# Projecting q and k in blocks of 128 columns, with DMAs that place the heads

## The chip, the cores and the metric

The kernel runs on one core of a Trainium2 chip. The metric is the device time of one execution in microseconds (us). In the core, TensorE (PE in the profile) multiplies matrices, ScalarE (ACT) takes exponentials, VectorE (DVE) and GpSimd (POOL) do elementwise work, and SyncE (SP) only issues DMAs. PSUM, where matmuls write, has eight banks of 128 x 512 fp32. Each engine works through its own instructions in a fixed order and waits on semaphores where it needs another's result.

## The reference, cut to what matters

```python
# x: 2048 x 640, 32 heads of 20
q, k, v = split(x @ wqkv)
o = softmax(q @ k.T / sqrt(20)) @ v          # per head, 2048 x 2048 scores
a = o @ wo
h = x @ w1 + b1                              # 2048 x 1536
b = (h * tanh(softplus(h))) @ w2             # "mish"
g = sigmoid((x * gate_w).sum(-1))
out = g * a + (1 - g) * b
```

The exponentials of the scores, 32 x 2048 x 2048, are by far the most elementwise work.

## The kernel before

The whole instruction order is written by a planner in Python. `Plan.add` (line 91) appends an instruction to an engine and keeps an estimated clock for each engine from the costs given (a DMA counts as done 2.0 us after its issue, line 45). Where the code decides what comes next, it does so by these estimated clocks; what comes out is a fixed program.

**Attention.** The work is cut into units (query chunk c of 512, group g of 4 heads, key tile kt of 128, head j). Three units make a slot; there are 683 slots, and the main loop (line 1037) has one step for each. A step issues the exponential of its slot (`emit_e`, line 738, the ACT row L749), the scores of the slot two ahead (`emit_s`, line 715, L723), and products with v of older slots (`pv`, L822). A score matmul needs the exponential of two slots before to have left its banks. Keys and queries of a group lie in `KT` and `QT` as four heads of 20 rows, each padded to 32 rows, so that a head starts at a row divisible by 32. One group of 512 queries takes 16 key tiles, 21 1/3 slots. The first chunk of queries, c = 0, takes slots 0 to 170 and is called stage one below.

**Off units.** In some slots the third unit's exponential is taken off ACT: DVE evicts the scores (L763) and computes the exponential with a polynomial (L776 to L780). `choose` (line 788) picks them where DVE's queued work is small.

**Repeats.** Where PE would be busy for too small a share of a step, `repeat_s` (L733) issues the score matmuls a second time, to the same place.

**Fillers.** All other matmuls are tasks that share one PSUM bank, `FB`: each has some matmuls and then an eviction, almost always on DVE, which frees the bank. `tasks` is ordered by due step. A forced task whose due step has come is issued at the head of the step; otherwise, at the end of each step, `pick` (line 1002) may give a task that is ready, as long as PE's estimated clock stays within the end of the next exponential (line 1074). It gives nothing while the bank is not free at PE's estimated clock.

- `kq_task(k, g, c)`: q (k = 0) or k (k = 1) of group g for 512 rows of x: 5 matmuls of 512 columns (L402) with a weight in which the group's 80 columns are padded to 128. POOL or DVE copy the padded weights (`pad`, L391). One DVE cast (L422) writes the result to `QT` or `KT`, already in padded rows. There are 64 of them; k of all rows and q of the first chunk are due in stage one. k of chunk c is due 3 steps before the first slot that reads it.
- `v_task(g, c)`: v of a group, 20 small matmuls (L437), cast by L445; 32 of them, all in stage one.
- `sq_task(n)`: the guard. POOL squares x and the weights (L478), PE sums them over the rows (L491), DVE takes the maximum (L498). From the eight maxima a flag is set that decides whether a second, safe program has to run (it doesn't here). Due at steps 60 to 165.
- `h_task`, `b_task`, `p_task`: the dense branch and the output projection, from slot 171 on; `mish` between them uses ACT (L574), DVE and POOL. An `h_task` can start only when all eight sums are read, because they share the buffer `HB`.

**Norm.** When a group ends, DVE evicts the sums (L884) and SP issues three DMAs one after the other: `RR<-OUNG` (L887), after a reciprocal `SUMS<-RR` (L892), then `BCT<-SUMS` (L894), which spreads the reciprocals over the rows. DVE multiplies (L864) when that has landed.

**Start.** SP issues four transposing loads of x, one per 512 rows (L354). ACT issues the loads of the weights: the first group's columns at once, the others after the first part of x has landed. q and k of group 0 and chunk 0 are projected, the scores of slots 0 and 1 follow.

Of the kernel before, what the change touches and what calls it, by code (L numbers as in the profile page):

```python
# [166 lines left out]
def bass_gated_mix__softmax_full_mha__dense_activation_mish__prompt_kernel(  # L167
# [71 lines left out]
    PADK = REG[:, NFT * (2 * D + 2):].rearrange("p (b f c) -> p b f c", b=2, c=P)  # L239
# [12 lines left out]
    PADQ = WOQ[:, NFT * D:NFT * (D + 2 * P)].rearrange("p (b f c) -> p b f c", b=2, c=P)  # L252
# [20 lines left out]
    def attention(pl, fast):  # L273
# [70 lines left out]
        if fast:  # L344
# [17 lines left out]
            m_padq = pl.add("dve", lambda e: e.memset(PADQ, 0.0), cost=0.4)  # L362
            m_padk = pl.add("dve", lambda e: e.memset(PADK, 0.0), cost=0.4)
# [17 lines left out]
            pad_done, pad_read = {}, {}  # L381

            def pad(k, g, again):

                if (k, g, again) not in pad_done:
                    b = g % 2
                    src = (WQ, WK)[k][:, :, g * HD:(g + 1) * HD].rearrange("p f (j d) -> p f j d", d=DH)
                    dst = (PADQ, PADK)[k][:, b, :, :].rearrange("p f (j d) -> p f j d", d=32)[:, :, :, 0:DH]
                    load = w_load[("wq", "wk")[k] + ("0" if g == 0 else "")]
                    pad_done[(k, g, again)] = pl.add(  # L390
                        "dve" if g == 0 and not again else "pool", lambda e: e.tensor_copy(dst, src),  # L391
                        [(m_padq, m_padk)[k], load, pad_read.get((k, b))], cost=0.4 if g == 0 else 1.2)
                    (wq_read, wkv_read)[k].append(pad_done[(k, g, again)])
                return pad_done[(k, g, again)]

            def kq_task(k, g, c, due, forced=True):
                b = g % 2
                dst = (QT, KT)[k]
                pads = (PADQ, PADK)[k]

                def mm(f):
                    return lambda e, bank: e.matmul(  # L402
                        PS[:, bank, :], pads[:, b, f, :], xt(c)[:, f, :], start=(f == 0), stop=(f == NFT - 1))

                def finish(bank, last):
                    pad_read[(k, b)] = last
                    x_read[c].append(last)
                    (wq_read, wkv_read)[k].append(last)

                    if c == ((0, 1, NC - 1, NC - 1)[c] if k == 0 else NC - 1):  # L410
                        if g + 2 < NG:
                            pad(k, g + 2, min(c, 2) if k == 0 else 0)
                        elif k == 0 and c < 2:
                            pad(0, g + 2 - NG, c + 1)
                    first = k == 1 and g == 0 and c == 0
                    to = dst[:, g, c * CW:(c + 1) * CW]
                    if first:
                        h = CW // 2
                        ev = pl.add("act", lambda e: e.copy(to[:, 0:h], PS[:, bank, 0:h]), [last], cost=0.4)
                        k_more.append(pl.add("act", lambda e: e.copy(to[:, h:], PS[:, bank, h:]), [last], cost=0.4))  # L420
                    else:
                        ev = dve(lambda e: e.tensor_copy(to, PS[:, bank, :]), [last], 0.69)  # L422
                    (q_done, k_done)[k][(g, c)] = ev

                    if first:
                        return k_more[0]
                    return ev

                return Task([mm(f) for f in range(NFT)], PASS, finish, due,
                            lambda: [xt_load[c], pad(k, g, min(c, 2) if k == 0 else 0)], forced)  # L430

# [35 lines left out]
            def sq_src(n):  # L467
                return xt(n) if n < 4 else (WQ, WK)[(n - 4) // 2][:, :, n % 2 * HALF:(n % 2 + 1) * HALF]

            def square():  # L470
# [6 lines left out]
                after = [xt_load[n]] if n < 4 else [w_load[k] for k in (("wq", "wq0"), ("wk", "wk0"))[(n - 4) // 2]]  # L477
# [3 lines left out]
                if n >= 4:  # L481
                    (wq_read, wkv_read)[(n - 4) // 2].append(op)
                else:
                    x_read[n].append(op)

            def sq_task(n, due):

                w = CW if n < 4 else HALF
# [22 lines left out]
            def load_w1(n):  # L511

                k = n % 6
                assert len(sq_ops) == 8
# [4 lines left out]
            def load_w2():  # L519
                flush(lambda: "busy" not in ei_free.values())  # L520
                w2_load.append(pl.add("sp", lambda e: e.dma_start(
                    W2, B_w2.rearrange("(f p) c -> p f c", p=P)), [*ei_free.values()], "w2", cost=0.6))

            def load_wo():
                assert len(sq_ops) == 8
# [189 lines left out]
        def emit_s(s):  # L715
# [3 lines left out]
            for i, (c, g, kt, j) in enumerate(slots[s]):  # L719
                need = deps + ([k_done[(g, kt // 4)], q_done[(g, c)]] if fast else [])  # L720
# [34 lines left out]
        def emit_x(s):  # L755
# [8 lines left out]
                s_op[s], ei_free[b], *(wkv_read if c == 1 and g == 0 and n < 3 else ())], EVICT)  # L764
# [137 lines left out]
        if fast:  # L902
            pad(0, 0, 0)
            pad(1, 0, 0)
            for task, bank in [(kq_task(0, 0, 0, -1), 3), (kq_task(1, 0, 0, -1), 4)]:
# [9 lines left out]
            for c in range(1, NC):  # L915
                due = slot_of(0, 0, 4 * c)
                tasks.append(kq_task(1, 0, c, due - 3))
                tasks.append(v_task(0, c, due - 1))
            for g in range(1, NG):
                due = slot_of(0, g, 0)  # L920
                tasks.append(kq_task(0, g, 0, due - 5))
                for c in range(NC):
                    due = slot_of(0, g, 4 * c)
                    tasks.append(kq_task(1, g, c, due - 3))
                    tasks.append(v_task(g, c, due - 1))
            start = slot_of(1, 0, 0)
            last_kv = tasks[-1]
            for n in range(8):
                t = sq_task(n, 60 + 15 * n)
# [11 lines left out]
            qs = [(kq_task, (0, g, 1)) for g in range(NG)]  # L941
            qs += [(kq_task, (0, g, c)) for g in range(NG) for c in range(2, NC)]
# [19 lines left out]
            for t, (make, args) in zip(made, rest):  # L962
# [4 lines left out]
                if make is kq_task:  # L967
                    t.due = min(t.due, slot_of(args[2], args[1], 0) - 4)
# [12 lines left out]
        def flag_ops(last):  # L981
# [5 lines left out]
            a = pl.add("dve", lambda e: e.tensor_tensor(m[:, 0:1], m[:, 0:1], m[:, 1:2], ALU.max), [a])  # L987
            for n in (0, 2, 3):
                a = pl.add("dve", lambda e, n=n: e.tensor_tensor(
                    m[:, 0:1], m[:, 0:1], m[:, n:n + 1], ALU.mult), [a])  # L990
            f = pl.add("dve", lambda e: e.tensor_scalar(
                FLAG[0:1, 0:1], m[:, 0:1], (SAFE / (SCALE * DH)) ** 2, None, ALU.is_gt), [a])
# [9 lines left out]
        def pick():  # L1002

            if now["open"]:
                return now["open"]
            for t in tasks:
                more = t.ready()
                free = bank_free.get(FB)
                if free is not None and free.t1 + HOP + FREE > pl.now["pe"]:
                    return None  # L1010
                if more is not None and all(d is None or safe(d) <= pl.now["pe"] for d in more):
                    return t
# [24 lines left out]
        for step in range(NSLOT + 40):  # L1037
# [22 lines left out]
            if step + 2 < NSLOT:  # L1060
# [5 lines left out]
                if owed + rate > 0.1 and pick():  # L1066
# [9 lines left out]
            while owed > 0 and step < NSLOT:  # L1076
                t = pick()
# [139 lines left out]
```

## Time and profile before

| | |
|---|---|
| median of 3 runs (lowest, highest) | 967.91 us (965.39, 973.04) |
| the profiled execution | 968.21 us, of which 966.4 us are the profile's span |
| ACT busy | 920.5 us, 95% of the span |
| PE busy | 799.7 us, 83% |
| DVE busy | 614.4 us, 64% |
| POOL busy | 397.3 us, 41% |
| granted PE clock, mean | 0.964 |

A row of a group of instructions names the line, the engine, the operation and what it writes and reads; then how often, the sum of busy time and the mean of one instruction in ns; after the bar the idle time of the engine just before these instructions and what ended most of it. Instructions overlap in their pipelines: the mean of one is longer than the pace at which they follow each other. The five matmuls of a `kq_task`, at 395 ns each, pass in 1.25 us.

### The profile page before, as it was taken

The numbers are of one execution on the slowest core, as the hardware profiler recorded it, in microseconds if no ns is written. First come the engines' busy times: TensorE is split into PE (matmuls) and PEld (weight loads), VectorE is DVE, ScalarE is ACT, GpSimd is POOL, SyncE is SP. The second block draws the span as 40 slices with busy tenths as digits, with TensorE's granted clock in tenths as the row PEclk, the third lists the DMA queues.
The fourth block names the chain that finished last, engine by engine and source line by source line (L and its number), as shares of the span: only waits on it lengthen the run. The fifth ranks groups of instructions, "written<-read, shape, count | busy, mean of one in ns | idle before, by whom it ended". The sixth has DMA issues, their size and how long they took to land.

```text
span 966.4 us, 16483 instructions
## 1 busy us (share of the span) xinstructions
PE 799.7 (83%) x6886; PEld 260.9 (27%) x6886; DVE 614.4 (64%) x1006; ACT 920.5 (95%) x738; POOL 397.3 (41%) x465
## 2 busy tenths in 40 slices
PE   8888889888888888888878888877887888787985
PEld 3332233333222122222222222222222222222221
DVE  2356765565677577656666667775767755757645
ACT  5999999999999889999999999999999999999995
POOL 2400243120266456605355557156556525656100
PEclk9998999999999889999999999999999999999798
DMA  9000000000310111200111111011011011110000
GB/s 211 2 13 13 12 13 2 12 13 26 121 42 27 38 35 44 49 28 25 53 47 46 35 40 39 26 54 51 24 40 53 12 54 33 49 39 13 12 12 31
DMA packets 63137, 35.98 MB, mean 37 GB/s; under 512 B 22225, under 2 KB 59089, under 8 KB 63057
## 3 DMA queue, kind: packets, MB, share of 16 engines
q1 hardware_dynamic: 59040, 32.40, 12.0%
q10 hardware_dynamic: 3936, 2.46, 0.9%
q8 instruction: 56, 0.92, 0.4%
q14 instruction: 25, 0.20, 0.1%
q0 software_dynamic: 80, 0.00, 0.0%
HBM read 29.10 MB, written 2.88 MB: 33 GB/s over the span
## 4 chain that ended last, share of the span: by engine, by line
ACT 67%; PE 13%; DMA 10%; DVE 7%; issue 2%; POOL 1%; ACTq 0%; POOLq 0%
ACT ETS L749 65%; DMA BCT<-SUMS 5%; PE PS L723 4%; DMA SUMS<-RR 3%; PE PS L402 3%; PE PS L822 2%; ACT REG L574 2%; PE PS L543 2%; DVE ER L779 1%; DMA XB<-in_A_x_dram 1%; PE PS L733 1%; DVE OTN L864 1%; DMA RR<-OUNG 1%; PE PS L616 1%; DVE OFF L780 1%
## 5 line engine op out<-in xcount | busy, mean ns | idle before, releaser
L749 ACT ACTIVATE ETS<-PS 128x1536 bf16<-128x1536 f32 (+1 forms) x683 | 905.3, 1541 | 24.8 <-PE PS L723 17.8
L723 PE MATMUL PS<-QT,KT 32*128 32x512 bf16 x2048 | 275.3, 395 | 137.2 <-ACT ETS L749 126.4
L822 PE MATMUL PS<-ETS,V_all 128*21 128x512 bf16 x1980 | 210.3, 396 | 0.9 <-ACT ETS L749 0.9
L723 PEld LDWEIGHTS PS<-QT,KT 32*128 32x128 bf16 x2048 | 67.0, 91 | 360.3 <-ACT ETS L749 331.6
L583 POOL TENSOR_TENSOR T<-REG 128x256 f32<-128x256 f32 x48 | 43.8, 913 | 214.4 <-DVE REG L588 214.4
L779 DVE SCALAR_TENSOR_TENSOR ER<-ER,EM 128x512 f32<-128x512 f32 x136 | 108.4, 797 | 1.9
L583 POOL TENSOR_TENSOR T<-T 128x128 f32<-128x128 f32 x96 | 69.8, 727 | 51.9 <-DVE T L599 46.3
L822 PEld LDWEIGHTS PS<-ETS,V_all 128*21 128x21 bf16 x1980 | 49.3, 89 | 141.2 <-issue 133.6
L733 PE MATMUL PS<-QT,KT 32*128 32x512 bf16 x650 | 85.5, 386 | 0.0
L543 PE MATMUL PS<-XB,REG 128*128 128x256 bf16 x480 | 79.3, 287 | 4.9 <-DVE QT L422 2.6
L583 POOL TENSOR_TENSOR REG<-REG,T 128x256 f32<-128x256 f32 x96 | 79.2, 825 | 7.5
L616 PE MATMUL PS<-W2R,HB 128*128 128x320 bf16 x384 | 77.8, 311 | 3.4 <-DVE XB L623 1.9
L583 POOL TENSOR_TENSOR REG<-REG 128x256 f32<-128x256 f32 x96 | 77.2, 804 | 7.5
L553 DVE TENSOR_TENSOR HB<-PS,B1F 128x512 bf16<-128x512 f32 x48 | 33.0, 688 | 50.3 <-PE PS L543 50.2
L763 DVE TENSOR_SCALAR REG<-PS 128x512 int32<-128x512 f32 x51 | 35.1, 689 | 45.9 <-PE PS L723 37.4
L583 POOL TENSOR_TENSOR HB<-REG,HB 128x512 bf16<-128x512 f32 x48 | 58.7, 1223 | 3.8
L779 DVE SCALAR_TENSOR_TENSOR ER<-EM 128x512 f32<-128x512 f32 x68 | 52.4, 771 | 0.8
L640 PE MATMUL PS<-WOQ,OTN 128*128 128x320 bf16 x256 | 49.4, 307 | 2.9 <-DVE OTN L864 1.5
L402 PE MATMUL PS<-XB,WOQ 128*128 128x512 bf16 x160 | 47.6, 396 | 3.9 <-DVE QT L422 2.1
L543 PEld LDWEIGHTS PS<-XB,REG 128*128 128x128 bf16 x480 | 38.7, 100 | 44.1 <-issue 40.3
L599 DVE RECIPROCAL T<-T 128x128 f32<-128x128 f32 x48 | 45.3, 944 | 6.8 <-POOL T L583 6.8
L391 POOL COPY WOQ<-WOQ 128x400 bf16<-128x400 bf16 x23 | 13.0, 566 | 88.7 <-PE PS L402 80.6
(79 smaller groups left out, 702.7 us busy)
## 6 DMA issues: line engine op xcount, KB each, us to landing
REG<-in_B_w_dram SPq DMA_DIRECT2D x48, 320.0 KB, 3.2
BCT<-SUMS SPq DMA_DIRECT2D x31, 256.0 KB
W2R<-in_B_w_dram SPq DMA_DIRECT2D x1, 1920.0 KB, 10.6
out_dram<-OUTT SPq DMA_DIRECT2D x12, 160.0 KB, 1.8
REG<-in_A_wqkv_dram ACTq DMA_DIRECT2D x2, 700.0 KB, 5.8
WOQ<-in_A_wo_dram SPq DMA_DIRECT2D x4, 200.0 KB
WOQ<-in_A_wqkv_dram ACTq DMA_DIRECT2D x1, 700.0 KB, 8.5
out_dram<-ETS SPq DMA_DIRECT2D x4, 160.0 KB, 3.1
```

Of the source, the lines that this page charges most:

```text
L402: return lambda e, bank: e.matmul(PS[:, bank, :], pads[:, b, f, :], xt(c)[:, f, :], start=(f == 0), stop=(f == NFT - 1))
L543: return lambda e, bank: e.matmul(PS[:, bank, i * HW:(i + 1) * HW], W1B[:, n1 % 2, f, i * P:(i + 1) * P], xt(c)[:, f, cols], start=(f == 0 ...
L583: last[0] = pl.add("pool", lambda e: e.tensor_tensor(out, x, y, ALU.mult), [last[0], *deps], cost=cost)
L599: last[0] = pl.add("dve", lambda e: e.reciprocal(T2[:, :], T2[:, :]), [of4], cost=0.95)
L616: return lambda e, bank: e.matmul(PS[:, bank, 0:HALF], HB[:, hc % 2, f, t * P:(t + 1) * P], W2[:, f, half * HALF:(half + 1) * HALF], start ...
L640: return lambda e, bank: e.matmul(PS[:, bank, 0:HALF], OTN[:, c % 2, g, t * P:(t + 1) * P], WOG[:, g, half * HALF:(half + 1) * HALF], star ...
L723: last = pl.add("pe", lambda e, i=i, c=c, g=g, kt=kt, j=j: e.matmul(scores(s)[:, i, :], KT[32 * j:32 * j + 32, g, kt * P:(kt + 1) * P], QT ...
L733: s_op[s] = pl.add("pe", lambda e, i=i, c=c, g=g, kt=kt, j=j: e.matmul(scores(s)[:, i, :], KT[32 * j:32 * j + 32, g, kt * P:(kt + 1) * P], ...
L749: e_op[s] = pl.add("act", lambda e: e.activation(ETS[:, s % NETS, 0:n, :], scores(s)[:, 0:n, :], AF.Exp, scale=SCALE), [s_op[s], pv_slot.g ...
L763: ev_op[s] = dve(lambda e: e.tensor_scalar(x, scores(s)[:, 2, :], SCALE * LOG2E, BIAS, ALU.mult, ALU.add), [s_op[s], ei_free[b], *(wkv_rea ...
L779: piece(0.69, lambda e, i=i: e.scalar_tensor_tensor(r, r if i else m, POLY[i], m, ALU.add, ALU.mult))
L822: return pl.add("pe", lambda e: e.matmul(PS[32 * j:32 * j + EW, ACC, :], V_all[:, kt, h, :], src, start=(count == 0), stop=(count == NKT - ...
```

## The change

q and k are projected in five blocks of 128 real columns instead of eight groups of 80 padded ones: 38 tasks `kq_task(k, b, c)`. A block's 128 columns hold six or seven heads and parts, in rows that are not the padded ones. DVE casts the block to one of three staging buffers, `STG`, and SP issues one DMA for each head or part of a head, 20 rows (or 8, 12, 16, 4) of 1 KB, to its padded rows in `KT` or `QT`. Since these DMAs write only the 20 rows of a head, POOL first clears `KT` and `QT` (`clear`), in an order written out before the loop, on the same queue as two of the padded weight copies. The first two groups of the first chunk are still projected with padded weights (`pad_task`, four of them). Scores wait for the last DMA of the blocks that their group needs. The due steps of the blocks are 5 (k) and 7 (q) slots before the first reader, instead of 3 and 5 (4 for later q).

The guard sums the weights first (due at steps 50 to 110) and x later (steps 170 to 188). `pick` is given a limit: it may give a task whose bank or inputs are not free yet, if they are by the estimated clocks in time for the task's first matmul to end within the limit; PE then waits in its place. The order of the later q tasks is by chunk, not by group.

```diff
+            def clear(k, g, c, n):
+                dst = (QT, KT)[k][:, g, c * CW:(c + n) * CW]
+                op = pl.add("pool", lambda e: e.memset(dst, 0.0), cost=0.45 * n)
+                zero.update({(k, g, i): op for i in range(c, c + n)})
...
+            def pad_task(k, g, due):
+                to = (QT, KT)[k][:, g, 0:CW]
...
+            def kq_task(k, b, c, due, forced=True):
...
                 def mm(f):
                     return lambda e, bank: e.matmul(
-                        PS[:, bank, :], pads[:, b, f, :], xt(c)[:, f, :], start=(f == 0), stop=(f == NFT - 1))
+                        PS[:, bank, :], w[:, f, b * P:(b + 1) * P], xt(c)[:, f, :], start=(f == 0), stop=(f == NFT - 1))
...
+                    r = stage[0] % 3
+                    stage[0] += 1
+                    ev = dve(lambda e: e.tensor_copy(STG[:, r, :], PS[:, bank, :]), [last, *stage_read[r]], 0.69)
+                    done = (q_done, k_done)[k]
+                    op = None
+                    groups = set()
+                    for h in range(H):
+                        lo, hi = max(h * DH, b * P), min((h + 1) * DH, (b + 1) * P)
+                        if lo >= hi or (h < 2 * HG and c == 0):
+                            continue
+                        g, j = divmod(h, HG)
+                        groups.add(g)
+                        to = t[32 * j + lo - h * DH:32 * j + hi - h * DH, g, c * CW:(c + 1) * CW]
+                        op = pl.add("sp", lambda e, lo=lo, hi=hi, to=to: e.dma_start(
+                            to, STG[lo - b * P:hi - b * P, r, :]), [ev, zero[(k, g, c)]], f"st{r}", cost=0.07)
+                    stage_read[r] = [op]
+                    wq_read.append(op)
+                    for g in groups:
+                        done.setdefault((g, c), []).append(op)
...
+                            lambda: [xt_load[c], w_load[name], w_load[name + "0"]], forced)
...
-                need = deps + ([k_done[(g, kt // 4)], q_done[(g, c)]] if fast else [])
+                need = deps + ([*k_done[(g, kt // 4)], *q_done[(g, c)]] if fast else [])
...
+            pad(0, 0)
+            pad(1, 0)
+            clear(1, 0, 1, 3)
+            pad(1, 1)
+            pad(0, 1)
+            clear(1, 1, 1, 3)
+            for g in range(2, NG):
+                clear(1, g, 0, NC)
+                clear(0, g, 0, 1)
+            for g in range(NG):
+                clear(0, g, 1, 3)
...
+            first_of = [0, 1, 3, 4, 6]
+            todo = []
+            for c in range(NC):
+                for g in range(NG):
+                    if c or g:
+                        todo.append(v_task(g, c, slot_of(0, g, 4 * c) - 1))
+                for b in range(c == 0, 5):
+                    g = first_of[b] + (b == 1 and c == 0)
+                    todo.append(kq_task(1, b, c, slot_of(0, g, 4 * c) - 5))
+            for k in range(2):
+                todo.append(pad_task(k, 1, slot_of(0, 1, 0) - 3 - 2 * (k == 0)))
+            for b in range(1, 5):
+                todo.append(kq_task(0, b, 0, slot_of(0, first_of[b] + (b == 1), 0) - 7))
+            tasks += sorted(todo, key=lambda t: t.due)
...
-                t = sq_task(n, 60 + 15 * n)
+                t = sq_task(n, 50 + 20 * n if n < 4 else 170 + 6 * (n - 4))
...
+        def pick(limit):
+
+            switch = SWITCH if pl.kind != "F" else 0
             if now["open"]:
-                return now["open"]
+                return now["open"] if pl.now["pe"] + now["open"].cost + switch <= limit else None
+            free = bank_free.get(FB)
+            begin = max(pl.now["pe"] + switch, free.t1 + HOP + FREE if free is not None else 0)
             for t in tasks:
+                if begin + t.cost > limit:
+                    return None
                 more = t.ready()
-                free = bank_free.get(FB)
-                if free is not None and free.t1 + HOP + FREE > pl.now["pe"]:
-                    return None
-                if more is not None and all(d is None or safe(d) <= pl.now["pe"] for d in more):
+                if more is not None and all(d is None or safe(d) + t.cost <= limit for d in more):
                     return t
...
-                if owed + rate > 0.1 and pick():
+                if owed + rate > 0.1 and pick(pl.now["pe"] + 0.8):
```

## The prediction

> **What bounds the kernel now.** First the busy shares and the costliest groups, with forms kept apart:
>
> ```profile
> ACT 67%; PE 13%; DMA 10%; DVE 7%; issue 2%; POOL 1%; ACTq 0%; POOLq 0%
> ...
> L749 ACT ACTIVATE ETS<-PS 128x1536 bf16<-128x1536 f32 x614 | 852.8, 1583 | 24.4 <-PE PS L723 17.5 <-PE PS L733 6.8
> L749 ACT ACTIVATE ETS<-PS 128x1024 bf16<-128x1024 f32 x69 | 79.2, 1163 | 0.4 <-PE PS L723 0.3
> ```
>
> ACT is busy 95% of the span and holds two thirds of the chain that ended last. Of its 45.9 us idle, 24.8 stand before L749 and wait for scores; the rest is start (first exponential at 12.54 us) and tail. So the change can win only these 24.8 us, and what ACT sheds: an off unit shortens an exponential by 1583 - 1163 = 420 ns. PE time as such is worth nothing.
>
> Next, where the 24.8 us stand. ACT's waits cut at 244 us (the end of stage one) give 7.0 + 4.2 = 11.2 us for L749 before and 14.3 after. The stage in windows of 8 us shows two kinds (columns: length, then busy us and count of PE, PEld, DVE, ACT and POOL, granted clock, DMA share, GB/s):
>
> ```profile
> 200.00:208.00 8.00, 6.01 (x62) 2.28 (x62) 6.75 (x11) 6.45 (x6) 5.29 (x5) 1.00 0.00 1
> 320.00:328.00 8.00, 6.52 (x35) 1.32 (x35) 5.85 (x10) 5.33 (x4) 1.28 (x3) 0.57 0.00 0
> 352.00:360.00 8.00, 5.44 (x35) 1.63 (x34) 4.79 (x7) 5.36 (x5) 4.57 (x6) 0.65 0.01 3
> 896.00:904.00 8.00, 8.00 (x50) 1.71 (x48) 5.59 (x11) 7.36 (x7) 2.98 (x4) 0.50 0.02 2
> ```
>
> Nearly all of ACT's loss after 244 us lies in windows where the clock was below 1; in stage one some 9 of 11 us lie in windows at full clock. There it goes as at 200 us in the timeline:
>
> ```profile
> 195.47 0.54 SPq L894 DMA_DIRECT2D BCT<-SUMS  x1
> 200.72 0.69 DVE L864 TENSOR_TENSOR OTN<-OUNG,BCT 128x512 bf16<-128x512 f32 x1 [1.23 <-DMA BCT<-SUMS]
> 201.93 0.47 DVE L498 TENSOR_REDUCE MXS<-PS 1x1 f32<-1x320 f32 x1
> 202.46 0.90 PE L437 MATMUL PS<-REG,XB 128*128 128x80 bf16 x20 [1.32 <-DVE MXS L498]
> 203.72 2.79 ACT L749 ACTIVATE ETS<-PS 128x1536 bf16<-128x1536 f32 x2 [1.55 <-PE PS L723]
> ```
>
> A norm DMA lands late, DVE stands, the filler bank is freed late, PE stands before the next filler, the scores behind it are late. In stage one PE waited 3.7 + 2.7 us for the guard's evictions (L498) in 8 places, and for no q, k or v eviction in its list of waits.
>
> **Start: a loss.** It is read from SP's queue and the DMAs' issue and landing times:
>
> ```profile
> 0.75 19.67 SPq L354 DMA_TRANSPOSE XB<-in_A_x_dram  x4
> 12.54 26.97 ACT L749 ACTIVATE ETS<-PS 128x1536 bf16<-128x1536 f32 x20 [0.22 <-PE PS L723]
> 18.85 0.52 POOL L391 COPY WOQ<-WOQ 128x400 bf16<-128x400 bf16 x1 [8.04 <-DMA WOQ<-in_A_wqkv_dram]
> ```
>
> SP issues transposes until 20.42; the last lands at 16.9 + 7.1 = 24.0. Exponentials follow at (26.97 - 1.45) / 19 = 1.343 us, so that of slot 5, the first to read k of chunk 1, began at 12.54 + 5 x 1.343 = 19.26. Before, this k came from group 0's own early weights and a DVE cast at 17.54. Now it needs all of wk (issued 9.7, landed 16.4), a cast, and 7 DMAs on SP behind the transposes. The bulk weights and the clear of group 1, which POOL issues only after the wq copy of 18.85 (0.52 us, and 1.3 for the clear: 20.7), are ready about when SP is. One small DMA holds SP for 0.33 (SUMS<-RR) to 0.55 us (RR<-OUNG, the only SBUF to SBUF row), the planner's 0.07 notwithstanding: 7 take 2.3 to 3.9. Landing: 1.4 (SUMS<-RR) to 2.4 (an RR<-OUNG issued at 72.11 let SUMS<-RR out at 74.96; less 0.24 reciprocal and hops). Add 0.45 for score matmul and hop: exponential 5 at 24.6 to 27.2, middle 25.9. **Loss 5.3 to 7.9; taken 6.6.** ACT can't fill it, since slots go in order.
>
> What follows is late too. From a block's first pass to landed rows: 1.25 PE + 0.1 + 0.69 cast + 2.3 to 3.9 issue + 1.4 to 2.4 landing = 5.7 to 8.3 us; a due step 5 slots ahead covers 5 x 1.343 = 6.7. Run at its due step, a k block costs ACT 0 to 1.6. The first groups do run at due: casts at 17.54, 23.61 and 30.91 stand against due steps 2, 7, 13 = 15.2, 21.9, 30.0. Five more chunks of groups 0 and 1: 0 to 8, **taken 2.4**, since the planner spreads fillers to end 3 steps early where it can. Later groups have that lead; nothing there.
>
> [...]
>
> **Stage one: a gain.** After the start, fillers were 31 k, 7 q, 31 v and 8 sums = 77. They become 19 k and 4 q blocks, 2 padded, 31 v, 4 sums = 60, 22% fewer. Half the sums' evictions go, the kind PE waited for. Of 11.2 us ACT waits I take 40% away: **-4.5** (0 to -9). The floor is nothing, because the new `pick` lets PE stand for a bank where the old one passed it over, and a late DVE then costs as before. Passes go from 320 to 210; at 1.25 us per five that is 27 us of PE, and repeats (L733, 144 matmuls here) may fill it again; no gain from it.
>
> **DVE.** Casts by DVE go from 63 to 41: 22 x 0.69 = 15.2 us. One off unit takes 0.69 + 0.42 + 0.42 + 0.77 + 2 x 0.80 + 0.71 = 4.6 us; 15.2 buys 3.3 units of 0.42 = **-1.4** (0 to -2.8, twice that).
>
> **Later stages.** q goes from 24 tasks to 15 where they mix with the dense branch, 244 to 410 us, half of the 14.3 us: **-1** (-3 to +3, since the clock decides there). x's sums move to steps 170 to 188, so the dense branch starts some 15 us later than its first ACT row at 257.6; it ended at 886 of 956, so 70 us hide this. Uncovered, it would be those 15.
>
> **SP and POOL.** 36 DMAs for each chunk of q or k, 27 for the first: 2 x (27 + 3 x 36) = 270; 162 in stage one, 53 to 89 us of SP. Seven norm chains issue 21 DMAs through that queue; each meets a batch with chance about 0.3 and waits about 1.4: 9 us, in which DVE may stand on a landing, as it did for 9.8 us there. Over the span DVE stood 37.4 us before L864 and ACT waited 24.8 in all, so at most 0.66 of a DVE wait reaches ACT; I take a sixth, since ACT's 24.8 have other causes too: **+1.5** (0 to +6). The casts wait for a staging buffer of three tasks before: nothing. POOL clears 60 x 512 columns at 4.36 / 10 (the memset of L526) = 26 us, to about 45 us, where it was idle; the first sum is due at step 50 = 80 us. Uncovered, a block would wait for its clear, as above.
>
> **Sum.** 6.6 + 2.4 - 4.5 - 1.4 - 1 + 1.5 = +3.6 on 968.21 (span 966.4 and 1.8 around it) = 971.8; the median shown is 0.3 lower: **971.5**. All low ends: 5.3 - 9 - 2.8 - 3 = -9.5, 958.4. All high ends: 7.9 + 8 + 3 + 6 = +24.9, 992.8.
>
> **Rivals.**
> 1. *The filler bank was the trouble.* 17 fewer fillers and a `pick` without gaps end the bursts: stage one's waits fall by 9, the later by 5, off units by 2.8, start 6.6: 958. For it: PE's waits sit on that bank. Against: the waits begin with norm DMAs, which stay.
> 2. *Latency is met all along (slower).* Blocks run at their due step not only at first, and each of 19 k blocks brings 0.8 us more (middle of 0 to 1.6): 15 on ACT in place of 2.4; with the rest of the sum 984. It decides from the point where cast to landing exceeds 6.7 - 1.25 us. For it: 0.07 planned against 0.33 to 0.55. Against: the lead of 3 steps.
> 3. *The change doesn't do what it says for the time:* fewer passes are replaced by repeats, waits stay as they are: 6.6 + 2.4 + 1.5 - 1.4 = 977.
>
> **Chances.** Forecast 0.45 (own range 964 to 978), rival 1 0.17, rival 2 0.2, rival 3 0.18. Range 958 to 985: it takes in the low ends and rival 2's middle, and leaves out about 2 in 10. One per cent, about what can be told from no change, is 9.7: under 958.2, half of rival 1 and little else, 0.12; over 977.6, rival 2, nearly half of rival 3 and the forecast's upper end, 0.33; between, 0.55.
>
> **What would show it.** Exponential 5 at about 26 us, ended by a DMA; staging DMAs of 0.33 to 0.55 us on SP; L749's waits before 244 us from the filler bank down to 6 or 7 beside the start's; off units 70 to 75; first L574 near 272 us. Wrong I'd be where score matmuls wait for staging DMAs after 60 us (rival 2), where L749's waits after 30 us fall under 10 (rival 1), or where the clock falls in more windows than before.

## The result, and the profile after

The changed kernel takes 1038.36 us (1035.77 to 1045.02, 4 runs) beside 966.65 us (962.34 to 973.04) for the kernel before on the same chip: a ratio of 1.0747, 95% interval 1.0665 to 1.0828. It is slower by some 72 us; forecast were 971.5 us in a range of 958 to 985. The profiled execution took 1040.18 us with a span of 1038.4 us, against 968.21 and 966.4.

The page of the changed kernel: instructions, busy shares, busy tenths of ACT and the granted PE clock in 40 slices, the engines' shares of the chain, and the exponentials' group.

```profile
span 1038.4 us, 16328 instructions
PE 823.5 (79%) x6689; PEld 254.4 (24%) x6689; DVE 594.2 (57%) x983; ACT 925.2 (89%) x738; POOL 406.6 (39%) x460
...
ACT  3666889887976999889999999999999999999896
...
PEclk8778889887988999879999999998888999999798
...
ACT 56%; PE 16%; DMA 12%; DVE 6%; SPq 5%; issue 2%; POOL 1%; ACTq 0%
...
L780 ACT ACTIVATE ETS<-PS 128x1536 bf16<-128x1536 f32 (+1 forms) x683 | 909.3, 1549 | 91.7 <-PE PS L754 71.7
```

ACT does what it did before (925.2 us busy against 920.5, 683 exponentials), but waits 91.7 us for scores instead of 24.8. SP's queue, absent from the chain before, holds 5% of it. The digits put the loss in the first 13 of the 40 slices, which end at 337 us; the clock falls there too. The stages in windows (length; busy us and count of PE, PEld, DVE, ACT, POOL; granted clock, DMA share, GB/s):

```profile
16.00:60.00 44.00, 33.48 (x216) 9.25 (x216) 4.94 (x8) 26.15 (x19) 33.04 (x33) 0.66 0.18 47
60.00:110.00 50.00, 36.33 (x308) 12.79 (x305) 17.72 (x32) 32.97 (x25) 0.00 (x0) 0.81 0.07 18
110.00:210.00 100.00, 82.70 (x800) 29.25 (x799) 49.73 (x88) 90.13 (x69) 19.30 (x20) 0.93 0.09 24
210.00:330.00 120.00, 84.39 (x714) 25.93 (x713) 58.19 (x110) 93.93 (x75) 17.43 (x17) 0.83 0.16 47
```

Before, ACT was busy 43.48, 45.92, 95.16 and 115.74 us in these four windows, at clocks of 1.00, 0.93, 1.00 and 0.97. Added up from ACT's list of waits, the waits before exponentials are:

| waits before exponentials, us | until 110 us | 110 to 330 us | after 330 us |
|---|---|---|---|
| before | 4.8 | 9.0 | 10.8 |
| after | 36.8 | 35.6 | 18.3 |

The differences, 32.0 + 26.6 + 7.5 = 66.1, and 4.7 us more of busy time are all but 1.2 us of the 72.0 by which the spans differ.

**The first place: scores wait for staged rows.** From the timeline of the changed kernel (start, duration, engine, line and operation, how often, and in brackets the idle time just before and what ended it):

```profile
16.73 2.29 PE L433 MATMUL PS<-XB,REG 128*128 128x512 bf16 x5 [4.56 <-DMA REG<-in_A_wqkv_dram]
...
19.06 0.69 DVE L441 CAST WOQ<-PS 128x512 bf16<-128x512 f32 x1 [5.88 <-PE PS L433]
...
19.78 5.40 SPq L452 DMA_DIRECT2D KT<-WOQ  x7
...
20.04 4.14 ACT L780 ACTIVATE ETS<-PS 128x1536 bf16<-128x1536 f32 x3 [6.13 <-PE PS L764]
...
26.39 0.61 PE L754 MATMUL PS<-QT,KT 32*128 32x512 bf16 x2 [2.05 <-DMA KT<-WOQ]
...
27.04 1.45 ACT L780 ACTIVATE ETS<-PS 128x1536 bf16<-128x1536 f32 x1 [2.86 <-PE PS L754]
```

PE stands 4.56 us before the first block of k, because the block needs the whole of wk; the scores of slot 2 are queued behind it, and ACT waits 6.13. The five matmuls then take 2.29 us instead of 1.25. SP needs 5.40 us to issue seven DMAs, and the scores of slot 5 wait for the last of them. From the end of the cast (19.75) to those scores it is 6.6 us, and the cast itself is 0.69. This doesn't end with the start; PE's list of waits, each with its total, number and longest:

```profile
PE PS L754 <- DMA KT<-WOQ: 22.1, 8, 4.1
...
PE PS L574 <- DVE WOQ L441: 9.9, 3, 9.4
...
PE PS L433 <- DVE MXS L529: 6.5, 1, 6.5
...
PE PS L468 <- DVE V_all L476: 5.0, 1, 5.0
```

In the kernel before no score matmul waited for a DMA. The first row is the staging DMAs, seven of its eight waits by 105 us (21.7 us of the 22.1).

**The second place: the norm stands behind SP's batches.** The timeline of the changed kernel at 170 us:

```profile
170.86 0.61 SPq L918 DMA_DIRECT2D RR<-OUNG  x1
...
174.13 0.23 DVE L922 RECIPROCAL RR<-RR 128x16 f32<-128x16 f32 x1
174.23 5.15 SPq L452 DMA_DIRECT2D KT<-WOQ  x7
179.43 0.51 SPq L923 DMA_DIRECT2D SUMS<-RR  x1
181.01 0.59 SPq L925 DMA_DIRECT2D BCT<-SUMS  x1
...
185.91 0.69 DVE L895 TENSOR_TENSOR OTN<-OUNG,BCT 128x512 bf16<-128x512 f32 x1 [6.36 <-DMA BCT<-SUMS]
...
187.39 1.18 PE L468 MATMUL PS<-REG,XB 128*128 128x80 bf16 x15 [4.97 <-DVE V_all L476]
...
189.17 2.86 ACT L780 ACTIVATE ETS<-PS 128x1536 bf16<-128x1536 f32 x2 [4.83 <-PE PS L754]
```

The reciprocal is done at 174.36, but `SUMS<-RR` goes out only when the batch of seven has been issued, 5 us later. DVE reaches its multiply and stands 6.36 us; behind it on DVE is the cast that frees the filler bank; PE stands 4.97 before its next filler, and ACT 4.83. It is the chain that the prediction showed at 200 us of the kernel before, where DVE's wait was 1.23 us.

### The profile page after: what moved, and what is told of

Its sections match the earlier page's. It is cut to its first block, busy times and chain, and to the rows that moved or that the text cites. A ratio compares the mean times of both kernels' runs of the same rounds, so it can differ in the third digit from the quotient of the medians.

```text
span 1038.4 us, 16328 instructions
## 1 busy us (share of the span) xinstructions
PE 823.5 (79%) x6689; PEld 254.4 (24%) x6689; DVE 594.2 (57%) x983; ACT 925.2 (89%) x738; POOL 406.6 (39%) x460
## 3 DMA queue, kind: packets, MB, share of 16 engines
q1 hardware_dynamic: 66540, 37.32, 13.1%
## 4 chain that ended last, share of the span: by engine, by line
ACT 56%; PE 16%; DMA 12%; DVE 6%; SPq 5%; issue 2%; POOL 1%; ACTq 0%
ACT ETS L780 54%; DMA BCT<-SUMS 5%; PE PS L754 5%; SPq L452 5%; PE PS L853 3%; PE PS L433 2%; DMA SUMS<-RR 2%; ACT REG L605 2%; DMA RR<-OUNG 2%; PE PS L647 2%; DMA KT<-WOQ 1%; PE PS L468 1%; PE PS L764 1%; PE PS L574 1%; DMA WOQ<-in_A_wqkv_dram 1%
## 5 line engine op out<-in xcount | busy, mean ns | idle before, releaser
L780 ACT ACTIVATE ETS<-PS 128x1536 bf16<-128x1536 f32 (+1 forms) x683 | 909.3, 1549 | 91.7 <-PE PS L754 71.7
L754 PE MATMUL PS<-QT,KT 32*128 32x512 bf16 x2048 | 288.5, 412 | 148.8 <-ACT ETS L780 108.0
L853 PE MATMUL PS<-ETS,V_all 128*21 128x512 bf16 x1980 | 220.4, 414 | 0.6 <-DVE OUNG L915 0.6
L574 PE MATMUL PS<-XB,REG 128*128 128x256 bf16 x480 | 86.2, 289 | 14.6 <-DVE WOQ L441 9.9
L614 POOL TENSOR_TENSOR T<-T 128x128 f32<-128x128 f32 x96 | 65.9, 686 | 65.9 <-DVE T L630 59.5
L647 PE MATMUL PS<-W2R,HB 128*128 128x320 bf16 x384 | 82.1, 319 | 10.4 <-DVE XB L654 3.7
L764 PE MATMUL PS<-QT,KT 32*128 32x512 bf16 x563 | 79.6, 415 | 0.0
L509 POOL TENSOR_TENSOR HB<-XB 128x512 bf16<-128x512 bf16 x20 | 23.2, 1192 | 111.8 <-PE PS L522 111.8
L895 DVE TENSOR_TENSOR OTN<-OUNG,BCT 128x512 bf16<-128x512 f32 x31 | 24.8, 799 | 65.1 <-DMA BCT<-SUMS 64.8
L441 DVE CAST WOQ<-PS 128x512 bf16<-128x512 f32 x38 | 26.2, 689 | 54.8 <-PE PS L433 54.8
L671 PE MATMUL PS<-WOQ,OTN 128*128 128x320 bf16 x256 | 53.5, 307 | 2.6 <-DVE OTN L895 0.9
L810 DVE SCALAR_TENSOR_TENSOR ER<-EM 128x512 f32<-128x512 f32 x68 | 53.8, 791 | 0.8
L574 PEld LDWEIGHTS PS<-XB,REG 128*128 128x128 bf16 x480 | 36.3, 100 | 66.4 <-issue 63.3
```

The costliest lines, as they stand in the source:

```text
L574: return lambda e, bank: e.matmul(PS[:, bank, i * HW:(i + 1) * HW], W1B[:, n1 % 2, f, i * P:(i + 1) * P], xt(c)[:, f, cols], start=(f == 0 ...
L614: last[0] = pl.add("pool", lambda e: e.tensor_tensor(out, x, y, ALU.mult), [last[0], *deps], cost=cost)
L647: return lambda e, bank: e.matmul(PS[:, bank, 0:HALF], HB[:, hc % 2, f, t * P:(t + 1) * P], W2[:, f, half * HALF:(half + 1) * HALF], start ...
L671: return lambda e, bank: e.matmul(PS[:, bank, 0:HALF], OTN[:, c % 2, g, t * P:(t + 1) * P], WOG[:, g, half * HALF:(half + 1) * HALF], star ...
L754: last = pl.add("pe", lambda e, i=i, c=c, g=g, kt=kt, j=j: e.matmul(scores(s)[:, i, :], KT[32 * j:32 * j + 32, g, kt * P:(kt + 1) * P], QT ...
L764: s_op[s] = pl.add("pe", lambda e, i=i, c=c, g=g, kt=kt, j=j: e.matmul(scores(s)[:, i, :], KT[32 * j:32 * j + 32, g, kt * P:(kt + 1) * P], ...
```

## The experiments

Two causes are to be told apart for each place: that the placing of heads costs SP's time and latency (theory A), or that the rest of the change does (the choice of fillers, the guard's order, the blocks themselves).

### One DMA for each block

```diff
-                        op = pl.add("sp", lambda e, lo=lo, hi=hi, to=to: e.dma_start(
-                            to, STG[lo - b * P:hi - b * P, r, :]), [ev, zero[(k, g, c)]], f"st{r}", cost=0.07)
+                    to = t[:, (0, 2, 3, 5, 7)[b], c * CW:(c + 1) * CW]
+                    op = pl.add("sp", lambda e: e.dma_start(to, STG[:, r, :]), [
+                        ev, *(zero[(k, g, c)] for g in sorted(groups))], f"st{r}", cost=0.07 * n)
```

The heads are not placed in their rows, so the scores are of other numbers. `n` counts the DMAs for which the one stands, so the planner's estimates and the order on every engine are unchanged; the bytes on SP's queue are nearly so (37.38 MB beside 37.32).

> The changed kernel, with one DMA for each block of 128 columns in place of six to eight: it carries the same 128 KB from the staging buffer to rows of one group of the block, so the heads are not placed and that part of the computation is left out; the planner's estimated clocks, and with them the order on every engine, are those of the changed kernel. Theory A (SP's time: 0.71 to 0.75 us for each of 210 staging DMAs delays the blocks themselves and the norm's DMAs behind them): six of seven issues go, some 4.5 us per block; ACT's waits before the exponentials fall from 91.7 to 35 to 45 us, and the time to 975 to 995 us. What stays is the start (the block waits for the whole of wk and for the transposes on SP). Rival B (PE stands before fillers that the new pick takes too early, and its clock falls): DMAs don't matter much, over 1025 us. Rival C (the way of a block through staging is long by landing, not by issue): 1010 to 1030 us, with score matmuls still waiting for staging DMAs some 15 us in all.

Measured: 973.92 us (965.75 to 977.82, 8 runs) beside 970.32 before, ratio 1.0032 (1.0002 to 1.0063), just under theory A's range; its waits before exponentials, 22.4 us, are well under the 35 to 45 expected. The group of k's staging DMAs in this run (ns min/median/max), and then in the changed kernel:

```profile
L453 SPq DMA_DIRECT2D KT<-WOQ x19: 464/472/558, 21.1 to 194.1; - x19
```

```profile
L452 SPq DMA_DIRECT2D KT<-WOQ x135: 554/706/1516, 19.8 to 241.4; - x135
```

One issue of 0.47 us stands in place of seven of 0.71. Some 64 of the 72 us are gone: no score matmul waits for a staging DMA any more, and the waits before exponentials are 7.9, 2.9 and 11.6 us in the three stages. So the loss is the placing in small DMAs; how much of it is their latency and how much their hold on SP, this run doesn't divide. The granted clock came back with it, to 0.88 from 16 to 60 us and 0.97 to 1.00 from 60 to 700 us, so the low clock, too, came with the placing. The profiled execution (span 964.0) was the fastest of the eight, so its waits are on the low side.

### Earlier due steps

```diff
-                    todo.append(kq_task(1, b, c, slot_of(0, g, 4 * c) - 5))
+                    todo.append(kq_task(1, b, c, slot_of(0, g, 4 * c) - 12))
...
-                todo.append(kq_task(0, b, 0, slot_of(0, first_of[b] + (b == 1), 0) - 7))
+                todo.append(kq_task(0, b, 0, slot_of(0, first_of[b] + (b == 1), 0) - 14))
```

> The changed kernel with the k blocks due 12 slots before the first reader instead of 5, q of the first chunk 14 instead of 7. If the blocks' own latency (some 9 us from first pass to landed rows against 6.7 us of 5 slots) is what costs, score matmuls' waits for staging DMAs fall from 22 us to under 8, the start apart, and the time to 995 to 1020 us. If the sheer time of SP, and what stands behind it, counts, or if the first two groups hold most of it, where nothing can be earlier: 1025 us or more.

Measured: 1010.5 us (1008.79 to 1012.21), ratio 1.0419 (1.0337 to 1.05). The wait of scores for `KT<-WOQ` is gone from PE's list, and some 28 of the 72 us with it: this is what the blocks' own latency cost, met at the due step. The start got worse in one place, since two blocks now stand ahead of slot 2:

```profile
18.59 1.91 PE L433 MATMUL PS<-XB,REG 128*128 128x512 bf16 x4 [6.05 <-DMA REG<-in_A_wqkv_dram]
...
24.68 5.48 ACT L780 ACTIVATE ETS<-PS 128x1536 bf16<-128x1536 f32 x4 [10.41 <-PE PS L764]
```

From 110 to 330 us the waits are still 30.4 us: DVE stood 25.0 us there for `BCT<-SUMS` and 12.8 for `RR<-OUNG`, of which 12.0 in one place, right behind the load of w2 (see the run with all three repairs).

### The norm's DMAs on another queue

```diff
-            got = pl.add("sp", lambda e: e.dma_start(
+            q = "pool" if fast and c == 0 else "sp"
+            got = pl.add(q, lambda e: e.dma_start(
```

and likewise for the other two DMAs of the chain, in the first chunk of queries alone.

> The changed kernel, with the three norm DMAs of each group of the first query chunk issued by POOL on its own queue, and nothing else changed. Theory A in its second half (norm DMAs stand behind batches of 5 us on SP, DVE then stands before the multiply, the filler bank and the scores follow): ACT's waits between 110 and 320 us, 35 us in the changed kernel, fall to 10 to 18 us, those before 110 us (37 us) stay: 1010 to 1022 us. Rival C (only the blocks' own way costs): no change, 1030 to 1042 us. A norm DMA issued by POOL may cost more than by SP (1.19 and 0.87 us for the two small ones that POOL issued before).

Measured: 1030.12 us, ratio 1.0602 (1.0547 to 1.0657). The waits from 110 to 330 us fell from 35.6 to 21.2, the first stage's stayed (36.3): the direction is right, but the 14.4 us are less than the 17 to 25 expected, and the time fell by only 8 us, to the edge of what was expected if only the blocks' own way costs (1030 to 1042). Of the difference, 5.7 us came back as waits of ACT for DVE before `mish` (L605, 6.2 us instead of 0.5).

### The planner told what a DMA costs

```diff
-                            to, STG[lo - b * P:hi - b * P, r, :]), [ev, zero[(k, g, c)]], f"st{r}", cost=0.07)
+                            to, STG[lo - b * P:hi - b * P, r, :]), [ev, zero[(k, g, c)]], f"st{r}", cost=0.75)
```

> The changed kernel, with the planner told that a staging DMA takes SP 0.75 us instead of 0.07; due steps unchanged. If the plan's wrong figure is what hurts (norm pieces and fillers are put where their DMAs have not landed), DVE's standing before the norm's multiply falls from 64.8 us to 40 and the time to 1000 to 1018 us. If SP's time itself is what hurts, the waits only move: 1025 to 1045 us.

Measured: 1037.1 us, ratio 1.0674 (1.0616 to 1.0732): no gain. DVE's wait for `BCT<-SUMS` fell from 64.8 to 37.4 us over the span, and the score matmuls' wait for `KT<-WOQ` rose from 22.1 to 42.5. Told the cost, the planner only moved the wait. The due steps are constants; that they, and not the planner's estimates, set when a block runs is my reading, which the run with earlier due steps supports.

### Rows of a DMA

```diff
+                        hi = min(hi, lo + 16)
                         to = t[32 * j + lo - h * DH:32 * j + hi - h * DH, g, c * CW:(c + 1) * CW]
```

The last four rows of each whole head are left out.

> The changed kernel with 16 of the 20 rows of each head placed; the last four rows of every head are left out of the scores, the number of DMAs stays. The one DMA of 128 rows took SP 0.47 us where the DMAs of 20 rows took 0.71 and those of 4, 8 and 12 rows 0.55 to 0.65. [...] If a small DMA costs 0.7 us whatever its rows, 1030 to 1042 us.

Measured: 1032.37 us, ratio 1.0644 (1.0563 to 1.0726), and 0.589 us for an issue:

```profile
L453 SPq DMA_DIRECT2D KT<-WOQ x135: 508/589/1781, 19.7 to 232.0; - x135
```

The time lies where I expected it for a hold of 0.7 us whatever the rows, but the hold did change, from 0.706 to 0.589 us; and 16 rows aren't as cheap as the 128 of the one-DMA run (0.472). The intervals of this ratio and of the changed kernel's (1.0665 to 1.0828) overlap, so no gain in time is shown. The changed kernel's own trace has DMAs of five sizes; SP's median hold was 0.62 us for 4 rows, 0.66 for 8, 0.72 for 12, 0.56 for 16 and 0.71 for 20. (The 0.55 to 0.65 that I had put down to 4, 8 and 12 rows were those of 16, 4 and 8.)

### The placing shared between two queues

```diff
+                        by = ("sp", "pool")[h % 2] if k == 1 or c == 0 else "sp"
-                        op = pl.add("sp", lambda e, lo=lo, hi=hi, to=to: e.dma_start(
+                        ops[by] = op = pl.add(by, lambda e, lo=lo, hi=hi, to=to: e.dma_start(
```

> The changed kernel, in the first query chunk with every second staging DMA issued by POOL instead of SP; all heads are placed. Theory A (the queue of 7 issues of 0.75 us): a block's issue falls from 5.2 to about 3 to 4 us (POOL needed 0.9 to 1.2 us for each of its two small DMAs), SP is free for the norm earlier: 995 to 1020 us. If what counts is landing, or DVE being slowed by POOL's issuing: 1025 us or more.

Measured: 1041.69 us, ratio 1.074 (1.0663 to 1.0817). This tells nothing of the sharing as such: POOL's DMAs stood behind all its clears, until 51 us, and ACT waited 23.9 us in one piece. From 110 to 330 us, where POOL was free, the waits were 21.8 instead of 35.6 us. POOL was held 0.507 us by one of its DMAs for k (median of 68, 52 of them of 20 rows).

### The old choice of fillers in the changed kernel

`pick` and its two callers as before the change; all else as changed.

> The changed kernel with the old pick (no task while its bank or inputs are not free). Theory A (the way of the blocks through SP): the loss stays, 1025 to 1050 us, perhaps more, since with the old projections the new pick was worth about 10 us. Rival B (the new pick makes PE stand in front of fillers that wait for late DMAs and for DVE, and turns a late landing into a late score): under 1010 us.

Measured: 1063.35 us, ratio 1.0964 (1.0846 to 1.1082). Score matmuls waited 53.8 us for `KT<-WOQ`, in 16 places. The new choice doesn't make the loss; it takes some 20 to 25 us off it (by the ratios, and by the times).

### The choice and the guard's order in the kernel before

The kernel before with the new `pick` and the new order of the guard's sums; q and k as before.

> The kernel before, with the other two parts of the change alone: the guard's sums of x at steps 170 to 188, and the new pick with its limit; projections as before, no staging. Theory A: SP has nothing more to do, so no loss: 958 to 972 us. Rival B (the new pick lets PE stand in front of fillers): ACT's waits of 24.8 us grow to 45 and more, 985 us or slower.

Measured: 960.56 us (957.0 to 963.74), ratio 0.9897 (0.9851 to 0.9943). The exponentials' group and the chain of its page:

```profile
ACT 77%; PE 7%; DMA 7%; DVE 5%; issue 2%; POOL 1%; ACTq 0%; POOLq 0%; DVEq 0%
...
L749 ACT ACTIVATE ETS<-PS 128x1536 bf16<-128x1536 f32 (+1 forms) x683 | 905.5, 1570 | 15.7 <-PE PS L723 8.6
```

15.7 us of waits instead of 24.8, and this beats both kernels. The two parts alone; first `pick`, with its callers:

```diff
-                if owed + rate > 0.1 and pick():
+                if owed + rate > 0.1 and pick(pl.now["pe"] + 0.8):
...
-                t = pick()
+                t = pick(limit)
```

> The kernel before with the new choice of fillers alone (a filler may start if what it waits for comes within the step's slack). With the guard's order as well it was 960.6. My prediction priced the new choice at nothing to a few us. The two changed kernels with and without it stand 25 us apart. Theory A: the gain of the pair is the choice's, 957 to 963. Rival: the pair's gain is the guard's order, and then this run is 966 to 972.

Then the order of the guard:

```diff
-                t = sq_task(n, 60 + 15 * n)
+                t = sq_task(n, 50 + 20 * n if n < 4 else 170 + 6 * (n - 4))
```

> The kernel before with the guard's order alone (squares of wq and wk first, those of x from due 170 on, W1 loads after the fourth). Theory A: 966 to 971, no difference from before, since the squares run on POOL and PE has time between; the pair's gain is the choice's. Rival: the guard's order is the gain, 957 to 963.

Measured: the choice alone 961.47 us, ratio 0.9916 (0.9885 to 0.9946); the guard's order alone 969.06 us, ratio 1.0012 (0.9993 to 1.0031), beside 968.28 before. The gain is the choice's; of the guard's order alone no gain can be seen.

### The start repaired, with one DMA for each block

K of group 0 for chunks 1 to 3 from padded weights as in the kernel before; heads not placed, as in the first run.

```diff
+            for c in range(1, NC):
+                todo.append(pad_task(1, 0, slot_of(0, 0, 4 * c) - 3, c))
...
-                    g = first_of[b] + (b == 1 and c == 0)
+                    g = first_of[b] + (b == 1 and c == 0) + (b == 0)
```

> The run with one DMA of 128 rows per block (973.9, heads not placed), with the start repaired: K of group 0 for all chunks from padded weights, block 0 of K due from group 1. Theory A: the 6 us wait ahead of slot 2 goes, and nothing else of the one-DMA run is left that the kernel before with the new choice of fillers and the guard's order (960.6) doesn't have, so 960 to 968: projecting 128 columns at a time gains nothing even where the placing of heads costs one DMA. If projecting by blocks does gain (fewer matmuls, 81 of 512 columns), it would show here: 950 to 957. If the one-DMA run's loss lies elsewhere: 970 to 975.

Measured: 976.57 us (971.98 to 977.86 in six runs, 986.91 in a seventh), ratio 1.0076 (1.004 to 1.0112), not better than the 973.92 without the repair. The wait ahead of slot 2 is gone; ACT ran without a stop from 11.45 to 42 us. Then it comes back:

```profile
55.80 2.31 PE L433 MATMUL PS<-XB,REG 128*128 128x512 bf16 x5 [0.79 <-DVE WOQ L441]
58.05 0.61 PE L755 MATMUL PS<-QT,KT 32*128 32x512 bf16 x3
...
58.70 6.39 ACT L781 ACTIVATE ETS<-PS 128x1536 bf16<-128x1536 f32 x5 [4.71 <-PE PS L755]
```

Blocks follow one another through the one filler bank, the five matmuls here in 2.31 us instead of 1.25, and the scores stand behind them. That the blocks need their PE time early, each with the first head it holds, is my reading of this; no run separates it. What the run does show: the start as I described it isn't what divides the one-DMA kernel from the 960.6 of the unchanged projection.

### All three repairs

Earlier due steps, the norm's DMAs on POOL, and K of group 0 from padded weights, with all heads placed: the three edits shown above, together.

> The changed kernel with three edits at once. First, the blocks' due slots 12 and 14 ahead of their scores, as in the run with earlier due slots (1010.5). Second, the norm's three DMAs of chunk 0 by POOL's queue. Third, K of group 0 is projected for chunks 1 to 3 with padded weights (three more tasks of five matmuls of 512 columns), as the kernel before did, and block 0 of K takes its due from group 1, so that no score of group 0 waits for the whole of wk, for a cleared row or for a staging DMA. Theory A (three separate losses: blocks met at their due, about 28 us; the norm's DMAs behind batches of staging issues and behind the load of W2, 10 to 20 us; the start, 6 to 9 us): the three add up, 975 to 992, with under 8 us of ACT's waits before 110 us. Rival (the losses share one cause, the hold on SP, and each edit only moves the wait to the next one in the line): 1000 to 1012, little under the run with earlier due slots. With all waits gone and the guard's order and the new choice of fillers kept, the floor is the 960 of the kernel before with those two alone.

Measured: 995.03 us (992.42 to 1001.28), ratio 1.0294 (1.0251 to 1.0336): nearer to theory A's 975 to 992 than to the rival's 1000 to 1012, and in neither. The start's repair and the norm's queue bring some 15 us together on top of the due steps' 28. Waits before exponentials are 14.1, 10.8 and 15.6 us, against 1.7, 5.5 and 8.4 in the kernel with the choice and the guard's order alone. Of what is left, one place at 272 us (timeline of this run):

```profile
266.15 0.45 SPq L552 DMA_DIRECT2D W2R<-in_B_w_dram  x1
266.54 0.58 POOL L925 DMA_DIRECT2D SUMS<-RR  x1 [2.23 <-DVE REG L808]
...
272.61 0.69 POOL L927 DMA_DIRECT2D BCT<-SUMS  x1 [5.49 <-DMA SUMS<-RR]
...
279.89 0.69 DVE L895 TENSOR_TENSOR OTN<-OUNG,BCT 128x512 bf16<-128x512 f32 x1 [10.11 <-DMA BCT<-SUMS]
...
282.14 0.63 ACT L605 ACTIVATE REG<-HC 128x512 f32<-128x512 bf16 x1 [6.37 <-DVE HC L588]
```

The load of w2 (1536 x 640 bf16, 1.97 MB) has just been issued, and the two small DMAs, though on another queue, let the next step go 5.49 and 6.6 us after their own issue had ended; at 181 us in the changed kernel it was 1.1 and 4.3. (A load of w1 went out right behind that of w2.) The changed kernel stalls at the same load at 309 us. DVE has evicted the sums at 304.51, but 15 staging DMAs take SP from 295.87 to 308.71, and then the load goes out right ahead of `RR<-OUNG`:

```profile
303.83 0.68 DVE L915 COPY OUNG<-PS 128x512 f32<-128x512 f32 x1
...
308.76 0.45 SPq L552 DMA_DIRECT2D W2R<-in_B_w_dram  x1
309.25 0.72 SPq L918 DMA_DIRECT2D RR<-OUNG  x1
...
317.38 0.25 DVE L922 RECIPROCAL RR<-RR 128x16 f32<-128x16 f32 x1 [11.74 <-DMA RR<-OUNG]
...
320.99 4.30 ACT L780 ACTIVATE ETS<-PS 128x1536 bf16<-128x1536 f32 x3 [9.14 <-PE PS L754]
```

So DVE's 11.74 us have two parts: SP issued the DMA 4.7 us late, and it then took 7.4 us to land. The load itself landed at 317.15. In the kernel before, the load went out at 240.16, 9.4 us ahead of `RR<-OUNG`, which then landed in under 2 us.

## Why the prediction was wrong

- **The step that failed: "One small DMA holds SP for 0.33 (SUMS<-RR) to 0.55 us".** It was priced by single DMAs of the norm; the staging DMA holds SP 0.71 us (median), at a pitch of 0.75 to 0.77. Seven take 5.1 to 5.4 us, not 2.3 to 3.9. In the first block it was 6.6 us from the end of the cast to the scores, issue and landing together, so from first pass to scores 1.25 + 0.1 + 0.69 + 6.6 = 8.6 us, against the lead of 6.7, and about 1 us more for the five matmuls at the granted clock of 0.50 (2.29 us instead of 1.25). Landing, taken as 1.4 to 2.4, was not the miss: it was 1.8 (the median of POOL's in the run with two queues).
- **"Later groups have that lead; nothing there": wrong**, and with it the 2.4 us for five chunks. It was rival 2, which I had put to decide where cast to landing exceeds 5.45 us. It is 0.69 + 6.6 = 7.3 in the first block. Score matmuls waited for staging DMAs until 105 us, the sign I had named for it. But its size was wrong too: its 0.8 us for a block made 984 us, 54 short of the measured time, and the due steps alone give back 28 us.
- **SP and the norm, +1.5 (0 to +6): the second large miss.** I let a norm DMA meet a batch with chance 0.3 and wait 1.4 us. A batch is 5.2 us long, three DMAs of a chain may each meet one, and DVE's queue holds the cast that frees the filler bank. Moving the chain's DMAs took 14.4 us off the waits from 110 to 330 us; the one-DMA run took 32.7. The stall at the load of w2, which I hadn't seen at all, is 9.14 of ACT's waits; SP's batch and the slow landing share it.
- **Start: right in size, half right in mechanism.** Exponential 5 came at 27.04, inside 24.6 to 27.2. But I had ACT wait once, before slot 5; 6.13 us of the wait stood before slot 2, since the block that waits for wk is ahead of those scores in PE's order. And the number is in part luck: the seven issues took 5.40 us where I allowed 3.9 at most, but SP began them at 19.78 instead of 20.42, and only 1.2 us passed from the end of the last issue to the scores, where I had added at least 1.4 + 0.45.
- **The clock.** PE stood 4.56 us, and the next five matmuls took 2.29 us instead of 1.25; the granted clock was 0.50 from 16 to 32 us and 0.66 from 16 to 60 us, where the kernel before had 1.00. My sum had no term for it. In the one-DMA run, with the same order of work, it was 0.88 from 16 to 60 us and 1.00 from 60 to 110 (0.81 in the changed kernel): the low clock came with the stalls. That the standing still brings it down was not shown by itself, nor what the clock added to the stalls.
- **Stage one, -4.5: a gain exists, but from the wrong part.** The new `pick`, which I had as the reason for no gain, gives 6.8 us in the kernel before and some 20 to 25 in the changed one. The fewer fillers give nothing that the runs could find: with the placing as cheap as one DMA, the blocks are still 13 us slower than the old projection with the same `pick` (973.92 against 960.56).
- **DVE, -1.4: nothing.** DVE's busy time fell from 614.4 to 594.2 us, but the exponentials of two units were 69 before and 69 after. **Later stages, -1:** +7.5 us of waits after 330 us; which part makes them wasn't separated.
- **Rival 1** (the filler bank) falls: PE's waits for that bank's evictions didn't end but grew; the three rows shown above are 21.4 us, and the longest row of this kind was 3.7 us before. **Rival 3** (repeats take up what the passes leave) falls as an account of the time, since the waits didn't stay as they were. But what it says of the repeats is seen: they went from 650 to 563 matmuls, yet the kernel before with the new `pick` and the new order has 485. Measured from there the blocks bring 78 repeats back for the 110 passes that they save.

What stays open is the last 34 us (38 by the ratios) between all three repairs (995.0) and the 960.6. 24.9 are waits before exponentials, spread over all stages, and 6.4 stand at the place at 272 us; no single part of it was taken away alone.

## What to carry to other kernels

Price a transfer by what its issue holds the queue, measured on a DMA of the same kind and shape: cutting one into seven multiplied that hold by eleven (5.2 us against 0.47), and whatever else uses the queue pays for it. Set due steps from the whole way, first matmul to last row landed; a planner that is only told the true cost moves the wait, while an earlier due step removes it. A change made of several parts may hide a gain in a loss: one part alone, `pick`, was worth 0.8% where the whole cost 7.5%.

## What the runs showed of the hardware that was not expected

- SP was held 0.472 us (median) by an SBUF to SBUF DMA of 128 rows of 1 KB, and longer by every smaller one in the changed kernel: 0.623 us for 4 rows, 0.658 for 8, 0.724 for 12, 0.558 for 16 and 0.707 for 20. POOL's queue, in the run with two queues, was held 0.507 by one of its DMAs for k, most of them of 20 rows. So SP's hold doesn't go by the bytes: it grows from 4 to 12 rows, 16 rows are the cheapest of the five sizes, and 128 rows are cheaper still. No run here shows why.
- Behind the load of w2 (1.97 MB), `RR<-OUNG` on the same queue was good for use only when the load had landed. It was issued 0.5 us after the load in the changed kernel and 4.6 us after it in the one-DMA run; the reciprocal that waited for it began at 317.38 and 251.70, and the load landed at 317.15 and 251.53. On POOL's queue, in the run with all three repairs, `SUMS<-RR` was ahead of the load, but not by much: the DMA on POOL that waited for it began at 272.61, 5.49 us after the end of its issue, and the load landed at 274.4.
